# Two stores moved behind five DMA transposes in SyncE's queue, and one buffer moved from one pool tag to another

## The chip, the cores and the metric

The kernel runs on one core of one Trainium2 chip. The metric is the device time of one execution in microseconds. The profile names the core's engines PE (TensorE matmuls; PEld are its weight loads), DVE (VectorE), ACT (ScalarE), POOL (GpSimd) and SP (SyncE, which only issues DMAs here). "SPq" is SyncE's queue of instructions, and a DMA "lands" when its semaphore reports that all of its data has been written.

## The reference

Sliding-window causal attention over 8 batches of 8 heads, 576 positions and 64 channels, and after it a feed-forward layer with the gate h cos(h) over all 4608 rows.

```python
scores = scale * np.matmul(q, k.transpose(0, 1, 3, 2))       # window of 64 positions, causal
attn = exp(scores - max); attn = attn / sum(attn)
x = matmul(attn, v)        # (8, 8, 576, 64), then rows of 512: (4608, 512)
h = x @ w_in               # 512 -> 2048
out = (h * np.cos(h)) @ w_out   # 2048 -> 512, float32
```

## The kernel before, in words

The 4608 rows are nine tiles of 512 rows (`MT`), numbered 0 to 8. One batch is nine blocks of 64 positions, so a tile of eight blocks straddles batches. For each tile the kernel runs, on TensorE, the second attention product (`values`, L428: `o_ps` from the transposed weights `wT` and `v`), the first feed-forward product (L496: `h_ps`, 256 matmuls in bf16), and the second one (L747: `out_ps`, and for the last three tiles a form with fewer products, L585). ScalarE takes the sine of `h_ps` (L731), VectorE multiplies (L734).

Between these, in the same stage, lies the attention of a later batch. TensorE makes the scores in two bursts (`burst_scores`, L327). For each group of four score blocks VectorE subtracts the mask and finds the maximum (`g_max`, L364), ScalarE exponentiates (`g_exp`, L376), VectorE takes the reciprocal of the sum (`g_inv`, L386), GpSimd or, for some groups, VectorE writes the normalised weights `w` (`g_norm`, L393), and a DMA transpose from SyncE's queue turns them into `wT` (`g_trans`, L412). A few groups are transposed on TensorE instead (L409, copied by VectorE). There are nine groups in the stage of a tile. In the stage of tile 2 five of them are written and transposed one after the other in its second half, and the five results are read by `values` of tile 3 at the stage's end; the other four follow.

The rest of the DMA work of a stage: GpSimd issues the loads of `q`, `k` and `v` (L186, L192). SyncE issues, besides the weight transposes, the transposes of whole batches of q and k (`turn_q`, `turn_k`, L243, three DMAs each, the "turns"), and two stores of 512 KB per tile (`store`, L505), each with 256 finished rows.

The order is written out by hand. Up to tile 0 it is a list of steps (`FIRST`). From tile 1 on a plan holds steps with a time: `at(time, fn, ...)` puts a step in, `pump(time)`, called after each piece of the matmuls, runs the steps due by then. The times are in units of the program, `T` = 32 of them to a tile; they order the instructions and are no microseconds. Each engine runs its own instructions in the order in which they were recorded; what they wait for are semaphores that follow from the tiles that they read and write.

Two pool tags matter. `out` holds the finished rows, 256 rows to a buffer: `load_plain` borrows two buffers at the start, each tile takes two (L740), and a buffer may be written again when the store that reads it has landed. `w` holds a group of normalised weights; its buffer may be written again when the transpose that reads it is done. The buffers of a tag are taken in rotation, three for `out` (`OUTS`, L40) and eight for `w` (L391).

Of the kernel before, what the change touches and what calls it, by code (L numbers as in the profile page):

```python
# [15 lines left out]
BF16 = mybir.dt.bfloat16  # L16
# [9 lines left out]
GF = 4  # L26
# [9 lines left out]
T = 2 * Q  # L36
LAGS = (0.2, 1, 3, 3.2, 3.8)
SKEW = 3
DIRECT = (0, 7, 8)
OUTS = 3  # L40
FILL = (6, 12)
BUSY = 8
NB = 5
# [31 lines left out]
def kernel(  # L75
# [23 lines left out]
    att = ctx.enter_context(tc.tile_pool(name="att", bufs=3))  # L99
# [26 lines left out]
    def bank(which, name):  # L126
        return ps.tile([128, 512], F32, tag=which, name=name)

    def copy(engine, out, in_):
        {"a": nc.scalar.copy, "p": nc.gpsimd.tensor_copy}.get(engine, nc.vector.tensor_copy)(out, in_)  # L130
# [40 lines left out]
    def load_plain(name):  # L171
        rows = moe.tile([128, 2, d_model], F32, tag="out", name="rows", bufs=OUTS).rearrange("p a f -> p (a f)")[:, 0:RC * D]
        st["rows", name] = rows
        nc.sync.dma_start(out=rows, in_={"q": q, "k": k}[name][0, 0:2].rearrange("h (p c) d -> (h p) (c d)", c=RC))
# [213 lines left out]

    def g_norm(n, engine="p"):
        (e, _), rden = st.pop(("e", n)), st.pop(("r", n))  # L390
        w = att.tile([128, GF, 128], BF16, tag="w", name="w", bufs=8)  # L391
        u = len(groups[n])
        (nc.gpsimd if engine == "p" else nc.vector).tensor_tensor(out=w[:, 0:u], in0=e[:, 0:u], op=ALU.mult,  # L393
                                in1=rden[:, 0:u].unsqueeze(2).to_broadcast([128, u, 128]))
        st["w", n] = w
# [86 lines left out]
    def put_out(m, engine=None):  # L482
        if ("osb", m // 2) not in st:
            st["osb", m // 2] = moe.tile([128, 2, d_model], F32, tag="out", name="out_sb", bufs=OUTS)
        copy(engine, st["osb", m // 2][:, m % 2], st.pop(("out", m)))

    def exp_table():
        nc.scalar.activation(small, small, AF.Exp, scale=0.0)
# [4 lines left out]
    def first(mt, ff, ks, start, stop):  # L493
        if start:
            st["h", ff] = bank(H_BANKS[mt == 1][ff], "h_ps")
        nc.tensor.matmul(out=st["h", ff], lhsT=w_in_sb[:, ks, ff * 128:ff * 128 + 128],  # L496
                         rhs=st["xT", mt][:, ks], start=start, stop=stop)

    def skewed(mt, ks, n):
        for ff in range(SKEW):  # L500
            first(mt, ff, ks, n == 0, n == PAIRS - 1)

    def store(o_sb, mt, ms0, e, n):
        r0 = mt * MT + (ms0 + e) * 128
        nc.sync.dma_start(out=out[r0:r0 + n * 128].rearrange("(a p) f -> p a f", p=128), in_=o_sb[:, e:e + n])  # L505
# [21 lines left out]
    def plan_rows(mt, gT):  # L527
        t = mt * T
        for f in range(4):
            at(t + (8 + 0.1 * f if mt == FAST[0] else 2 * f + 1.2), sum_row, 2, f, gT, "p")  # L530
            for i in range(2):
                at(t + (11, 13, 14.62, 14.7)[f] + 0.01 * i, sum_row, i, f, gT, "d")
            at(t + (18 if mt == FAST[0] else 17.7) + 0.01 * f, sum_row, 3, f, gT, "d")
        if mt < n_mt - 1:
            at(t + T - 0.505, sine_table)

    def fast_second(mt, gT):
# [7 lines left out]
        acc, temp = {}, {}  # L545
        o1, o2 = (moe.tile([128, 2, d_model], F32, tag="out", name="out_sb", bufs=OUTS) for _ in range(2))

# [51 lines left out]
    def at(time, fn, *args):  # L599
        plan.append((time, len(plan), fn, args))  # L600

    def pump(time):
        plan.sort(key=lambda x: x[:2])
        while plan and plan[0][0] <= time:
            _, _, fn, args = plan.pop(0)
            fn(*args)


    for i, (b, jobs, banks) in enumerate(bursts):
        t = T * (b - 1)  # L610
        at(t + (BURST[i % 2] + 0.9 * (i == 1) if b < B - 1 else (17.2, T + 14.6)[i % 2]), burst_scores, i)
        for n in range(jobs[0][0], jobs[-1][-1] + 1):
            place = (n - n_listed) % NU
            time = t + BURST[0] + PACE * place
            if b == B - 1:
                for time, fn in zip(LAST_STEPS[place], (g_max, g_exp, g_inv, g_trans)):
                    at(t + time, fn, n)
                at(t + LAST_STEPS[place][2] + 0.01, g_norm, n, "p")
                continue
            lags = LAGS[:2] + tuple(t + T - 0.79 - time + 0.01 * s for s in range(3)) if place == NU - 1 else LAGS  # L620
            if b == 2 and place > 3:
                lags = tuple(max(x, y - time) for x, y in zip(lags, {4: (53.2, 53.5, 0, 0, 0), 5: (0,) * 5, 6: (0, 0, 60.96, 60.97, 61.5), 7: (0, 0, 61.1, 61.2, 61.8), 8: (61, 61.3, 0, 0, 0)}[place]))
            for lag, fn in zip(lags, (g_max, g_exp, g_inv)):
                at(time + lag, fn, n)
            at(time + lags[3], g_norm, n, "d" if n == n_listed + 5 else "p")
            if n in last:
                at(T * b - 4.1 + (n == last[1]), g_trans, n)
                at(T * b - 4.05 + (n == last[1]), g_put, n)
            else:
                at(time + lags[4], g_trans, n)  # L630
# [51 lines left out]
    def spread_first(lo, hi):  # L682
# [16 lines left out]
             "s": lambda p, g, which: g_scores(2 * p + g, which), "m": lambda p, g: g_max(2 * p + g),  # L699
             "e": lambda p, g: g_exp(2 * p + g), "i": lambda p, g: g_inv(2 * p + g),  # L700
             "n": lambda p, g, engine: g_norm(2 * p + g, engine), "w": lambda p, g: g_trans(2 * p + g),
             "c": lambda p, g, engine: g_put(2 * p + g, engine), "v": values_half, "x": put_x_half,
             "tb": sine_table, "tb2": exp_table, "h": first_half, "S": sine_half, "g": gate_half,
# [9 lines left out]
    for mt in range(1, n_mt):  # L713
        base = mt * T
        gT = []
        if mt in FAST:
            plan_rows(mt, gT)
        for ks in range(PAIRS):
            pump(max([base - 1] + [time for time, _, fn, args in plan if fn is put_x and args[:2] == (mt, ks)]))
            skewed(mt, ks, ks)  # L720
        for ff in range(n_ff):
            for ks in range(PAIRS):
                if ff >= SKEW:
                    first(mt, ff, ks, ks == 0, ks == PAIRS - 1)
            h_ps = st.pop(("h", ff))
            sin = moe.tile([128, MT], F32, tag="sin", name="sin", bufs=4)
            if ff % 2 == 0:
                gt = moe.tile([128, 2, MT], BF16, tag="gT", name="gT", bufs=n_ff // 2 + 2)
                gT.append(gt)
            e = ff % 2  # L730
            nc.scalar.activation(sin, h_ps, AF.Sin, bias=math.pi / 2.0)  # L731
            if ff == n_ff - 1 and mt < B:
                exp_table()
            nc.vector.tensor_tensor(out=gt[:, e], in0=h_ps, in1=sin, op=ALU.mult)  # L734
            pump(base + ff)
        if mt in FAST:
            fast_second(mt, gT)
            continue
        for ms0 in range(0, MT // 128, 2):
            o_sb = moe.tile([128, 2, d_model], F32, tag="out", name="out_sb", bufs=OUTS)  # L740
            o_ps = [bank(which, "out_ps") for which in (("O1",) if mt == n_mt - 1 and ms0 else ("O1", "O0"))]
            for e in range(2):
                ms = ms0 + e
                for ff in range(n_ff):
                    if e and ms0 and ff == n_ff - 1 and 0 < mt < FAST[0]:
                        pump(base + T - 0.6)
                    nc.tensor.matmul(out=o_ps[e], lhsT=gT[ff // 2][:, ff % 2, ms * 128:ms * 128 + 128],  # L747
                                     rhs=w_out_sb[:, ff], start=ff == 0, stop=ff == n_ff - 1)
                    if ff % 4 == 3:
                        if ff == n_ff - 1:  # L750
                            copy("a" if e and (mt > 1 or ms0) else "d", o_sb[:, e], o_ps[e])
                            if mt == n_mt - 1:
                                store(o_sb, mt, ms0, e, 1)
                        pump(base + Q + 4 * ms0 + (e * n_ff + ff) // 4)
            if mt < n_mt - 1:
                at(base + T + 0.5 + ms0 / 2, store, o_sb, mt, ms0, 0, 2)


# [28 lines left out]
```

## Time and profile before

| | |
|---|---|
| runs shown | 299.11, 299.21, 297.6 us, median 299.11 |
| profiled execution, its own time | 296.92 us |
| its span | 295.2 us |
| granted TensorE clock | 1.00 throughout |
| DMA queues, share of 16 engines over the span | GpSimd's 83.5%, SyncE's 46.7% |
| HBM read, written | 36.70 MB, 9.44 MB |

Times inside the profile count from the start of the span. The stages of tiles 2, 3 and 4 begin at 87.01, 118.27 and 148.66 us. A row of the timeline gives the start, the length, engine and line, and what was written from what; behind it, in brackets, how long the engine had been idle and what ended that. A row of the DMA view gives what moved, the queue, how many issues the window holds, the size of one and the time from issue to landing.

### The profile page before, as it was taken

The numbers are of one execution on the slowest core, as the hardware profiler recorded it, in microseconds if no ns is written. First come the engines' busy times: TensorE is split into PE (matmuls) and PEld (weight loads), VectorE is DVE, ScalarE is ACT, GpSimd is POOL, SyncE is SP. The second block draws the span as 40 slices with busy tenths as digits, with TensorE's granted clock in tenths as the row PEclk, the third lists the DMA queues.
The fourth block names the chain that finished last, engine by engine and source line by source line (L and its number), as shares of the span: only waits on it lengthen the run. The fifth ranks groups of instructions, "written<-read, shape, count | busy, mean of one in ns | idle before, by whom it ended". The sixth has DMA issues, their size and how long they took to land.

```text
span 295.2 us, 8262 instructions
## 1 busy us (share of the span) xinstructions
PE 285.3 (97%) x2786; PEld 163.2 (55%) x2815; DVE 230.3 (78%) x906; ACT 238.0 (81%) x791; POOL 209.7 (71%) x230
## 2 busy tenths in 40 slices
PE   8979999999999999999999999999999999999995
PEld 3668854544454444444454545444547854884595
DVE  4998888887887876788678876996689878957853
ACT  5998699888987798879987999799977896937710
POOL 9999568992899759984999399948995476133200
PEclk9999999999999999999999999999999999999999
DMA  7999999999999999999999999999959415042013
GB/s 149 174 201 205 196 191 143 141 143 155 203 197 120 162 235 154 155 163 232 168 142 158 235 155 145 147 213 185 141 122 200 45 38 178 2 117 83 0 38 107
DMA packets 168267, 43.81 MB, mean 148 GB/s; under 512 B 155616, under 2 KB 163872, under 8 KB 168224
## 3 DMA queue, kind: packets, MB, share of 16 engines
q0 software_dynamic: 100896, 18.06, 83.5%
q1 hardware_dynamic: 67184, 25.15, 46.7%
q8 instruction: 22, 0.36, 0.5%
q14 instruction: 21, 0.17, 0.2%
q10 hardware_dynamic: 144, 0.07, 0.1%
HBM read 36.70 MB, written 9.44 MB: 156 GB/s over the span
## 4 chain that ended last, share of the span: by engine, by line
PE 86%; POOL 5%; ACT 3%; DMA 2%; issue 2%; DVE 1%; POOLq 0%
PE h_ps L496 38%; PE out_ps L747 18%; PE out_ps L585 13%; PE h_ps L460 5%; PE out_ps L479 5%; PE o_ps L428 3%; ACT e L376 2%; PE s_ps L327 2%; DMA wT<-w 2%; POOL v L192 1%; POOL q L169 1%; POOL k L169 1%; POOL w L393 1%; PE tw_ps L409 1%; PE s_ps L349 1%
## 5 line engine op out<-in xcount | busy, mean ns | idle before, releaser
L496 PE MATMUL h_ps<-xT,w_in 128*128 128x512 bf16 x502 | 111.3, 379 | 1.3 <-DVE xT L130 0.8
L393 POOL TENSOR_TENSOR w<-e,rden 128x512 bf16<-128x512 f32 (+1 forms) x68 | 69.2, 1030 | 48.6 <-DVE rden L386 38.6
L734 DVE TENSOR_TENSOR gT<-h_ps,sin 128x512 bf16<-128x512 f32 x128 | 84.6, 687 | 21.8 <-ACT sin L731 20.4
L376 ACT ACTIVATE e<-s,negm 128x128 f32<-128x128 f32 (+1 forms) x256 | 97.2, 382 | 2.6 <-DVE negm L364 1.6
L731 ACT ACTIVATE sin<-h_ps 128x512 f32<-128x512 f32 x128 | 73.6, 599 | 25.4 <-PE h_ps L496 23.5
L496 PEld LDWEIGHTS <-w_in 128*128 128x128 bf16 x512 | 50.2, 98 | 59.3
L747 PE MATMUL out_ps<-w_out,gT 128*128 128x512 bf16 x305 | 68.7, 379 | 1.1 <-issue 0.8
L364 DVE CUSTOM_DVE_ANT_0 s<-s_ps,mask 128x128 f32<-128x128 f32 (+1 forms) x256 | 55.8, 277 | 1.9 <-PE s_ps L349 1.6
L747 PEld LDWEIGHTS <-gT 128*128 128x128 bf16 x320 | 30.4, 98 | 35.5
L376 ACT ACTIVATION_READ_ACCUMULATOR e<-s,negm 128x1 f32 x256 | 48.0, 188 | 0.0
L192 POOL DMA_DIRECT2D v<-in_v_dram x40 | 34.1, 874 | 1.0 <-issue 0.9
L186 POOL DMA_DIRECT2D q<-in_q_dram x30 | 26.3, 894 | 3.6 <-issue 3.0
L186 POOL DMA_DIRECT2D k<-in_k_dram x30 | 26.3, 887 | 0.0
L386 DVE RECIPROCAL rden<-den 128x4 f32<-128x4 f32 (+1 forms) x73 | 12.0, 165 | 17.2 <-ACT e L376 16.8
L130 POOL COPY v<-v 64x1536 bf16<-64x1536 bf16 (+3 forms) x16 | 22.9, 1431 | 0.4
L364 DVE DVE_READ_ACCUMULATOR2_ANT negm<- 128x1 f32 x256 | 21.2, 83 | 0.0
L525 POOL TENSOR_TENSOR qT<-gT 128x512 bf16<-128x512 bf16 x12 | 13.6, 1154 | 9.1 <-DVE gT L734 9.0
L130 DVE CAST xT<-o_ps 128x512 bf16<-128x512 f32 x24 | 15.5, 680 | 5.8 <-PE o_ps L428 5.5
L585 PEld LDWEIGHTS <-gT 128*128 128x128 bf16 x152 | 14.0, 98 | 2.2
L460 PE MATMUL h_ps<-xT,w_in 128*128 128x256 bf16 x128 | 14.6, 273 | 0.0
L479 PE MATMUL out_ps<-w_out,gT 128*128 128x512 bf16 x60 | 14.3, 380 | 0.3 <-issue 0.2
L556 DVE TENSOR_TENSOR out_sb<-out_ps,p 128x512 f32<-128x512 f32 (+2 forms) x16 | 8.6, 548 | 6.7 <-ACT p L130 5.6
(90 smaller groups left out, 327.0 us busy)
## 6 DMA issues: line engine op xcount, KB each, us to landing
out_dram<-out_sb SPq DMA_DIRECT2D x16, 512.0 KB, 8.2
v<-in_v_dram POOLq DMA_DIRECT2D x32, 128.0 KB, 5.8
q<-in_q_dram POOLq DMA_DIRECT2D x24, 128.0 KB, 8.5
k<-in_k_dram POOLq DMA_DIRECT2D x24, 128.0 KB, 7.1
w_in<-in_moe_w_in_dram POOLq DMA_DIRECT2D x4, 512.0 KB, 9.4
w_out<-in_moe_w_out_dram POOLq DMA_DIRECT2D x4, 512.0 KB, 11.0
q<-in_q_dram POOLq DMA_DIRECT2D x7, 144.0 KB, 5.7
k<-in_k_dram POOLq DMA_DIRECT2D x7, 144.0 KB, 5.8
```

Of the source, the lines that this page charges most:

```text
L130: {"a": nc.scalar.copy, "p": nc.gpsimd.tensor_copy}.get(engine, nc.vector.tensor_copy)(out, in_)
L186: nc.gpsimd.dma_start(out=st[name, b][0:n, c].rearrange("p (h d) -> p h d", h=H), in_=src.rearrange("h p d -> p h d"))
L192: nc.gpsimd.dma_start(out=vt.rearrange("p (h d) -> p h d", h=H), in_=v[b, :, c * 128:c * 128 + n, :].rearrange("h p d -> p h d"))
L364: nc.vector.tensor_tensor_reduce(out=s[:, u, c], in0=s_ps[:, u, c], in1=mask[:, 2 - j % 2 if j else 0, c], scale=-scale if b else -1.0, sc ...
L376: nc.scalar.activation(e[:, u, c], s[:, u, c], AF.Exp, bias=negm[:, u:u + 1], scale=1.0 if n < n_first else -1.0, accum_out=den[:, u:u + 1])
L393: (nc.gpsimd if engine == "p" else nc.vector).tensor_tensor(out=w[:, 0:u], in0=e[:, 0:u], op=ALU.mult, in1=rden[:, 0:u].unsqueeze(2).to_br ...
L460: nc.tensor.matmul(out=h_ps[:, half * e:half * e + half], lhsT=w_in_sb[:, ks, ff * 128:ff * 128 + 128], rhs=st["xT", 0][:, ks, half * g:ha ...
L496: nc.tensor.matmul(out=st["h", ff], lhsT=w_in_sb[:, ks, ff * 128:ff * 128 + 128], rhs=st["xT", mt][:, ks], start=start, stop=stop)
L585: nc.tensor.matmul(out=to[n_] if split else to[:, e], lhsT=lhs[name][f // 2][:, f % 2, 128 * e:128 * e + 128], rhs=rhs[name][:, f, lo:hi], ...
L731: nc.scalar.activation(sin, h_ps, AF.Sin, bias=math.pi / 2.0)
L734: nc.vector.tensor_tensor(out=gt[:, e], in0=h_ps, in1=sin, op=ALU.mult)
L747: nc.tensor.matmul(out=o_ps[e], lhsT=gT[ff // 2][:, ff % 2, ms * 128:ms * 128 + 128], rhs=w_out_sb[:, ff], start=ff == 0, stop=ff == n_ff - 1)
```

## The change

The two stores of tile 1 get another time in the plan. Before, `at` gave them 0.5 and 1.5 units behind the end of tile 1's stage; now 24.2 and 24.22 units behind it, late in tile 2's stage. The other tiles' stores keep theirs. `out` gets four buffers in place of three and `w` seven in place of eight.

```diff
-OUTS = 3
+OUTS = 4
...
-        w = att.tile([128, GF, 128], BF16, tag="w", name="w", bufs=8)
+        w = att.tile([128, GF, 128], BF16, tag="w", name="w", bufs=7)
...
             if mt < n_mt - 1:
-                at(base + T + 0.5 + ms0 / 2, store, o_sb, mt, ms0, 0, 2)
+                at(base + T + (24.2 + 0.01 * ms0 if mt == 1 else 0.5 + ms0 / 2), store, o_sb, mt, ms0, 0, 2)
```

In SyncE's queue this is the stretch from the turns at the start of tile 2's stage to the turns for the batch after it. `wT<-w` are the weight transposes, the first three for the groups of the stage before, the next five those of tile 2's stage; `out_dram<-out_sb` are the stores.

```order
 L243 DMA_TRANSPOSE kT<-k 128x8x128 x2
 L243 DMA_TRANSPOSE kT<-k 128x4x64
-L412 DMA_TRANSPOSE wT<-w 128x4x128 x3
+L412 DMA_TRANSPOSE wT<-w 128x4x128 x8
 L505 DMA out_dram<-out_sb 128x2x512 x2
-L412 DMA_TRANSPOSE wT<-w 128x4x128 x5
 L243 DMA_TRANSPOSE qT_75<-q 128x8x128 x2
 L243 DMA_TRANSPOSE qT_75<-q 128x4x64
```

The two stores have moved behind the five transposes and stand directly ahead of the turns of q. This is the only difference in the order of any engine.

What instructions wait for changes in more places, since the buffers rotate otherwise. On VectorE, at the end of the written-out first part (two groups of batch 1 whose `w` VectorE writes itself), the rows with their semaphores are these; `DMAHW5` and `DMAHW6` count the landings of the first and the second weight transpose of the program.

```order
 L386 RECIPROCAL rden<-den 128x3 [waits Activation_49]
-L393 TENSOR_TENSOR w<-e,rden 128x384 [waits DVE_49]
-L384 MEMSET e 128x64 [waits Pool_49]
-L386 RECIPROCAL rden<-den 128x4 [waits Activation_49]
-L393 TENSOR_TENSOR w<-e,rden 128x512 [waits DMAHW5_49,DVE_49]
+L393 TENSOR_TENSOR w<-e,rden 128x384 [waits DMAHW5_49,DVE_49,Pool_49]
+L384 MEMSET e 128x64 [waits Pool_49]
+L386 RECIPROCAL rden<-den 128x4 [waits Activation_49]
+L393 TENSOR_TENSOR w<-e,rden 128x512 [waits DMAHW6_49,DVE_49]
 L130 COPY wT<-tw_ps 128x512 [waits PE_49]
 L130 COPY wT<-tw_ps 128x384 [waits PE_49]
```

The order is the same; each of the two writes now waits for one transpose later than before: the first, which waited for none, for the first, and the second for the second.

## The prediction

> **What bounds the kernel now.** I read the page first, then each tile's stage on its own, then the chain of waits around the one stage that is longer than its neighbours. The page says that TensorE is the bound.
>
> ```profile
> span 295.2 us, 8262 instructions
> PE 285.3 (97%) x2786; PEld 163.2 (55%) x2815; DVE 230.3 (78%) x906; ACT 238.0 (81%) x791; POOL 209.7 (71%) x230
> ```
>
> The span less the busy time leaves TensorE 9.9 us idle, so a change of the order of DMAs can gain only where TensorE waits for one. The windows of the stages of tiles 2, 3 and 4, each from the first h_ps matmul of a tile to that of the next (columns: window, its length, busy us and instruction count of each engine, granted clock, DMA share, GB/s), show where that is.
>
> ```profile
> 87.01:118.27 31.26, 30.34 (x261) 14.67 (x265) 23.14 (x109) 27.20 (x95) 26.19 (x29) 1.00 1.74 163
> 118.27:148.66 30.39, 29.97 (x260) 14.48 (x264) 23.21 (x109) 27.18 (x95) 24.69 (x27) 1.00 1.71 178
> 148.66:179.05 30.39, 29.97 (x260) 14.51 (x264) 23.18 (x109) 27.06 (x95) 25.00 (x27) 1.00 1.83 169
> ```
>
> Tiles 3 and 4 take 30.39 us; tile 2 takes 31.26, at the same clock of 1.00. The excess is 0.87 us. The chain of waits tells what ends last there (start, length, what):
>
> ```profile
> 110.91 1.05 POOL w L393
> ...
> 111.97 5.11 DMA wT<-w
> ...
> 117.13 0.98 PE o_ps L428 x50
> ...
> 147.37 1.13 PE o_ps L428 x64
> ```
>
> In tile 3's stage the 64 small o_ps matmuls run as one piece of 1.13 us. In tile 2's, TensorE stands still twice for a transposed weight block (the timeline; the bracket holds the idle time and what ended it):
>
> ```profile
> 116.04 0.38 PE L428 MATMUL o_ps<-wT,v 128*64 128x64 bf16 x11
> 116.61 0.22 PE L428 MATMUL o_ps<-wT,v 128*64 128x64 bf16 x3 [0.20 <-DMA wT<-w]
> 117.13 0.98 PE L428 MATMUL o_ps<-wT,v 128*64 128x64 bf16 x50 [0.29 <-DMA wT<-w]
> ```
>
> The last wait ends with the fifth weight transpose of the stage, which took 5.11 us from its issue at 111.97 to its landing.
>
> **The change: the two stores.** SyncE's queue in this stage and the next (start, length, what, how many):
>
> ```profile
> 100.55 1.10 SPq L505 DMA_DIRECT2D out_dram<-out_sb  x2
> 105.92 7.24 SPq L412 DMA_TRANSPOSE wT<-w  x5
> 113.33 5.58 SPq L243 DMA_TRANSPOSE qT<-q  x3
> 119.75 2.01 SPq L412 DMA_TRANSPOSE wT<-w  x1
> 121.87 4.73 SPq L243 DMA_TRANSPOSE kT<-k  x3
> 126.69 4.29 SPq L412 DMA_TRANSPOSE wT<-w  x3
> 131.08 1.15 SPq L505 DMA_DIRECT2D out_dram<-out_sb  x2
> ```
>
> The two stores, 1 MB together, stand ahead of the five transposes and will stand behind them. SyncE itself idles from 101.65 to 105.92, so their issue delays nothing today. Their data do. The DMA view of the windows around each issue gives the time to landing of the two stores, of the first transpose and of the fifth:
>
> ```profile
> out_dram<-out_sb SPq DMA_DIRECT2D x1, 512.0 KB, 8.6
> out_dram<-out_sb SPq DMA_DIRECT2D x1, 512.0 KB, 9.6
> wT<-w SPq DMA_TRANSPOSE x1, 7.1
> wT<-w SPq DMA_TRANSPOSE x1, 5.1
> ```
>
> The stores land at about 109.2 and 110.9 (100.55 + 8.6, 101.22 + 9.6), the first transpose only at 113.0 (105.92 + 7.1), the fifth at 117.1. They land in order. Two cuts through the DMA queues (packets, MB, share of 16 engines; q1 is SyncE's queue, q0 GpSimd's), for 105.3 to 109.2 and for 113 to 117:
>
> ```profile
> q1 hardware_dynamic: 614, 1.04, 82.2%
> q0 software_dynamic: 1012, 0.13, 50.3%
> ...
> q1 hardware_dynamic: 2177, 0.53, 140.6%
> q0 software_dynamic: 82, 0.01, 4.0%
> ```
>
> In the first 3.9 us q1 moves the stores' 1.04 MB and nearly nothing else, though transposes are issued from 105.92 on. In the second, q0 is empty and q1 works off the transposes. With the stores behind, the transposes find their queue free when issued, and the stores fall into the stretch in which q0 is empty.
>
> The Trainium skill ("DMA: Bandwidth & Descriptors", section "Queues, rings and completion order") says that each DMA engine takes the descriptors of one queue row in ring order, and changes between rows packet by packet. By that rule the transposes must wait for the stores of their own row, and the landings above agree; if an engine took turns within a row too, the move would be worth nothing and the sum would stay at 296.92.
>
> How early can the fifth land? It cannot be issued before GpSimd has written its block: that ends at 111.96 on the chain, whatever the stores do. So the gain hangs on its landing time alone. The nearest rows are the last transpose of the same run of blocks in tile 3's stage (issued at 141.69, itself behind two stores) and in tile 4's (issued at 172.14), and the extremes of all 60:
>
> ```profile
> 141.69 1.19 SPq L412 DMA_TRANSPOSE wT<-w  x1
> ...
> wT<-w SPq DMA_TRANSPOSE x1, 3.8
> wT<-w SPq DMA_TRANSPOSE x1, 2.5
> DMA to landing us min/median/max: 2.4/5.1/8.8
> ```
>
> TensorE reaches the block after 14 of its 64 matmuls, 14/64 of 1.13 = 0.25 us after 116.04: at 116.29, which is 4.3 us after the issue. At 3.8 us or less nothing waits; at an unchanged 5.1 it still waits 0.8. I take 3.8, since that transpose too had a store pair close ahead of it and three of its own kind; the bounds are 2.4 and 5.1. The second to fourth blocks are issued 4.4 to 1.4 us earlier and come first. The stage then lasts as long as tile 3's, to 87.01 + 30.39 = 117.40 in place of 118.27. **Gain: 0.87 us** (bounds 0.1 to 0.9).
>
> What is late next? The next stages run at 30.39 without a wait for DMA, so they begin 0.87 us earlier and keep it, unless the moved stores hurt them. Behind the stores now stand the three qT turns, one weight transpose and three kT turns. Their issue slips by 1.1 us, their data by up to the stores' 3.9. Their first user is the burst of scores of the next stage; its second part needs the last kT turn (its issue, its time to landing, and the two parts):
>
> ```profile
> 124.68 1.92 SPq L243 DMA_TRANSPOSE kT<-k  x1
> ...
> kT<-k SPq DMA_TRANSPOSE x1, 6.6
> 132.17 0.59 PE L327 MATMUL s_ps<-kT,qT 64*64 64x64 bf16 x32
> 137.98 0.86 PE L327 MATMUL s_ps<-kT,qT 64*64 64x128 bf16 x40
> ```
>
> The turn lands at 131.3, needed at 137.98 - 0.87 = 137.1: 5.8 us of cover against 3.9. The first part needs only the first turns of q and k, issued at 113.33 and 121.87, over ten us earlier. **Cost: nothing**; without that cover it would be up to 3.9 us. GpSimd's and ScalarE's queues issue the same in the same order.
>
> **Four row buffers, seven weight buffers.** With three row buffers tile 2's second pair would be copied into the buffer that tile 1's first store reads. With four, tile 1's buffers are needed next by tile 3, whose first copy stands here:
>
> ```profile
> 136.82 0.69 DVE L130 COPY out_sb<-out_ps 128x512 f32<-128x512 f32 x1
> ```
>
> A store issued at about 113.2 that takes as long as 9.6 us lands at 123: 13 us of cover. Nothing gained either, since today no copy waits for a store.
>
> With seven weight buffers a block waits for the transpose of the seventh before it, not the eighth. In the stages above these are most of a stage apart. It is close only at the end of the written-out first part, where VectorE writes two blocks and now waits there for the first and the second DMA transpose of the program (the run of six from 43.13, of which the second is issued at 44.45; then the second's time to landing, and the two VectorE blocks):
>
> ```profile
> 43.13 8.85 SPq L412 DMA_TRANSPOSE wT<-w  x6
> ...
> wT<-w SPq DMA_TRANSPOSE x1, 7.1
> ...
> 51.36 0.73 DVE L393 TENSOR_TENSOR w<-e,rden 128x384 bf16<-128x384 f32 x1
> 52.23 0.69 DVE L393 TENSOR_TENSOR w<-e,rden 128x512 bf16<-128x512 f32 x1
> ```
>
> The second lands at 51.55, 0.68 us before VectorE needs it; the first has no landing in the trace, but stands ahead in the queue, so it is there by 51.55, at the worst 0.2 us late. Behind these two in VectorE's queue are the copies that feed tile 1's first matmuls, so the cost is 0 to 0.2 us. I take 0, since 0.87 us separate the two VectorE blocks and 1.3 the two issues, which puts the first at about 50.3.
>
> Sum: the profiled execution took 296.92 us for a span of 295.2. 296.92 - 0.87 + 0 + 0 = 296.05. The three runs shown are 297.6 to 299.21, median 299.11; the profiled one lies below them all, so I take the difference to the median: 299.11 - 0.87 = **298.2 us**.
>
> **The rivals.**
>
> *The wait stays.* The transposes between 113 and 117 may be slow by themselves: there q1 needs 140.6% for 0.53 MB, where the stores needed 82.2% for 1.04 MB. If the fifth takes 5.1 us with a free queue too (the median of all 60), TensorE waits to 117.09 as now. For it speaks that median; against it the 3.8 and 2.5 at the same place of the next stages. Gain 0 to 0.1: 299.0 us. Chance 0.22.
>
> *The stores are paid for one stage later: slower.* The DMA engines are busy nearly throughout, so 3.9 us of stores, put behind, may push everything in q1 until tile 3's four blocks arrive late. The fourth lands at 141.69 + 3.8 = 145.5 and is needed 0.2 us into the o_ps that starts at 147.37, less 0.87: at 146.7. Cover 1.2 us. A full push of 3.9 makes TensorE wait 2.7: 299.11 - 0.87 + 2.7 = 300.9. It turns into a loss from a push of 1.2 + 0.87 = 2.1 us on. Against it: q0's 4.0% between 113 and 117 is a hole that the stores fill, and what q0 lost to them before 109 it gets back. Chance 0.10. The Trainium skill (same page, "Issuing engines are not separate DMA queues") says that DMAs from all issuing engines end on the same 16 engines and interleave, so that an order moves work and saves none; by it alone this rival would come first.
>
> *The shorter ring of weight buffers bites.* The cover of 0.68 us is one execution's. If the first transposes land 1 to 2 us later in others, VectorE stalls by 0.3 to 1.3 us ahead of tile 1: 299.11 - 0.87 + 0.3 to 1.3 = 298.5 to 299.5. Chance 0.08.
>
> **How the numbers follow.** The forecast has 0.60. A measurement of this kernel tells about 0.5% from no change, 1.5 us; no case gains that much, and only a strong push of the stores, over 2.1 + 1.5 = 3.6 us, loses it. The runs shown differ by 1.6 us among themselves, which I count as 0.12 for faster by over 0.5%. Slower gets half of the second rival and a rest, 0.06; within 0.5% keeps 0.82. Low end: the lowest run less the gain is 296.7, the profiled one less it 296.05; between them, 296.4. High end: the highest run with the buffer rival's loss, 299.21 + 0.4, and a part of the push: 299.9.
>
> **What would show it.** Right: tile 2's stage at 30.4 us, the five transposes at 2.4 to 4.3 us, no wait of o_ps for wT, the stores issued at about 113 and landing by 120, later stages at 30.39. Wrong: a stage of 31.2 with the fifth still at 5 us; a stage of tile 3 above 30.4 with o_ps waiting for wT or s_ps for kT; VectorE idle ahead of its two blocks near 52 us.

## The result, and the profile after

The changed kernel is slower. Six runs took 300.16 to 301.34 us, median 301.16, and six runs of the kernel before, recorded with them, had a median of 298.13: a ratio of 1.009, 95% interval 1.0062 to 1.0117. Here and below a ratio leaves out runs over 1.5% above the fastest of the same kernel and a median does not, so the two need not agree where such runs fall out (three of 12 with four loads, one of 12 in three other runs, and some of the kernel before). The forecast was 298.2 with a range up to 299.9. The rival in which the stores are paid for one stage later had been priced at 300.9 and given a chance of 0.10.

The page of the changed kernel shows 4.1 us more span (299.3 for 295.2). By it TensorE is busy for 4.7 us more (285.3 before) and idle for about as long as before.

```profile
span 299.3 us, 8285 instructions
PE 290.0 (97%) x2815; PEld 164.3 (55%) x2815; DVE 229.8 (77%) x906; ACT 238.2 (80%) x791; POOL 209.9 (70%) x230
```

This page alone would mislead, since matmul records are missing from a trace (2815 here, 2786 before), so the busy times of the two pages do not compare to a microsecond. The windows of the stages of tiles 2, 3 and 4, cut as before from the first h_ps matmul of a tile to that of the next, do (window, length, busy us and count of each engine, granted clock, DMA share, GB/s).

```profile
87.25:117.64 30.39, 30.39 (x265) 14.49 (x264) 23.14 (x109) 27.20 (x95) 25.33 (x28) 1.00 1.59 153
117.64:152.36 34.72, 31.67 (x265) 15.30 (x264) 23.91 (x111) 27.65 (x95) 29.52 (x32) 0.96 1.75 164
152.36:183.17 30.81, 30.81 (x265) 14.63 (x264) 22.51 (x107) 26.85 (x94) 21.15 (x23) 0.99 1.76 172
```

Tile 2's stage went from 31.26 to 30.39, the forecast gain of 0.87 us to the hundredth. Tile 3's went from 30.39 to 34.72, tile 4's to 30.81. The sum is -0.87 + 4.33 + 0.42 = +3.88; tile 2's stage also began 0.24 later, which no part of the change explains (in most of the runs below it begins 0.1 to 1.4 us later too), and together that is the 4.1.

TensorE at the end of tile 3's stage, in the timeline (start, length, what, how many, and in brackets the idle time before and what ended it):

```profile
146.67 0.69 PE L428 MATMUL o_ps<-wT,v 128*64 128x64 bf16 x12
148.48 0.19 PE L428 MATMUL o_ps<-wT,v 128*64 128x64 bf16 x1 [1.12 <-DMA wT<-w]
150.48 1.55 PE L428 MATMUL o_ps<-wT,v 128*64 128x64 bf16 x51 [1.81 <-DMA wT<-w]
```

It waits for two transposed blocks, 1.12 + 1.81 = 2.93 us. The 64 o_ps matmuls themselves take 0.69 + 0.19 + 1.55 = 2.43 us, where the piece quoted before took 1.13: 1.30 more. Of that 0.45 is what being broken up costs at a full clock: in tile 2's stage of the kernel before, with two waits in it, the same piece took 0.38 + 0.22 + 0.98 = 1.58 us. The rest is the clock. The 0.96 of the stage's row is an average: windows laid on the pieces give a granted clock of 1.00 for the first twelve matmuls and of 0.50 for the last 51, and 0.50 still from 152.03 to 152.57. Waits and slower matmuls make 4.23 of the 4.33 us; the other 0.1 is about what the half clock costs from 152.03 to the stage's end. The chain of waits through the same place (start, length, what) names the block, and shows the half clock go on into the next product, where 64 matmuls take 14.19 us for 13.83 in the stage before:

```profile
117.80 13.83 PE h_ps L496 x64
...
140.06 1.04 POOL w L393
...
141.89 8.54 DMA wT<-w
...
150.48 1.55 PE o_ps L428 x51
152.03 0.54 PE out_ps L747
152.57 14.19 PE h_ps L496 x64
```

The block was issued at 141.89, 0.2 us later than before (141.69), but took 8.54 us to land in place of 3.8. So GpSimd, which had written it by 141.10 (before: 141.66), is not late, and SyncE, which issues the transpose, hardly: the data are. SyncE's queue from the moved stores to that block:

```profile
97.41 16.05 SPq L412 DMA_TRANSPOSE wT<-w  x7
114.00 0.89 SPq L505 DMA_DIRECT2D out_dram<-out_sb  x2
115.06 6.95 SPq L243 DMA_TRANSPOSE qT<-q  x3
122.10 1.21 SPq L412 DMA_TRANSPOSE wT<-w  x1
123.41 5.57 SPq L243 DMA_TRANSPOSE kT<-k  x3
129.08 4.24 SPq L412 DMA_TRANSPOSE wT<-w  x3
133.42 1.12 SPq L505 DMA_DIRECT2D out_dram<-out_sb  x2
136.56 8.19 SPq L412 DMA_TRANSPOSE wT<-w  x4
```

The turns are issued 1.5 to 2.9 us later than before and the last kT turn lands at 134.8 (131.3 before), still ahead of its use. The two moved stores and the fifth transposition of tile 2's stage (DMA view) landed quickly, as forecast (3.8 us is the middle of 3.2 and 4.5):

```profile
out_dram<-out_sb SPq DMA_DIRECT2D x2, 512.0 KB, 3.8
...
wT<-w SPq DMA_TRANSPOSE x1, 2.4
```

What the prediction did not look at is the DMA engines' own row. For 109.5 to 114.5 us the DMA view gives the busy share of the 16 engines in 40 slices of 0.125 us, in tenths, and the queues' shares below it; first the kernel before, then the changed one.

```profile
DMA  9999999999999999999999999999999998910999
...
q0 software_dynamic: 2393, 0.30, 93.7%
q1 hardware_dynamic: 1782, 0.45, 84.8%
```

```profile
DMA  9999911099996999910699995000000199996100
...
q1 hardware_dynamic: 2484, 0.60, 86.2%
q0 software_dynamic: 68, 0.01, 2.9%
```

Before, no slice but three is below 9. After, there are holes. Counting a 9 as full and a digit d as (9.5 - d) tenths of a slice idle, the engines idle 0.24 us before and 1.91 us after. While the stores had gone first, GpSimd's loads (q0) had waited beside them and then filled the time in which q1 had little; with the stores held back, q0 is finished (2.9%), and q1 has nothing but transposes, each of which waits for GpSimd to write its block.

A second hole lies in tile 3's stage. This is the row from 135.25 to 139.25 in the changed kernel, in slices of 0.1 us; in the kernel before, 135.01 to 139.01 is 9 throughout:

```profile
DMA  9999999999999999999990001101115999999999
```

Counted in the same way, 135.25 to 143.25 holds 1.21 us of idle time, where 135.01 to 143.01 before holds 0.09, and this although tile 2's two stores had been issued at 133.42 and 134.08. They land at about 142.6 and 144.2. Before, they had landed by 141.2, ahead of the issue of the fourth block; now it is issued with their data still in its queue. GpSimd's loads, too, were out of the way before and are in it now (q0 for 143.01 to 147.01 before, then for 143.25 to 147.25 after):

```profile
q0 software_dynamic: 2, 0.00, 0.1%
...
q0 software_dynamic: 1552, 0.20, 76.9%
```

### The profile page after: what moved, and what is told of

Read it like the earlier page. It is cut to its first block, busy times and chain, and to the rows that moved or that the text cites. A ratio compares the mean times of both kernels' runs of the same rounds, so it can differ in the third digit from the quotient of the medians.

```text
span 299.3 us, 8285 instructions
## 1 busy us (share of the span) xinstructions
PE 290.0 (97%) x2815; PEld 164.3 (55%) x2815; DVE 229.8 (77%) x906; ACT 238.2 (80%) x791; POOL 209.9 (70%) x230
## 4 chain that ended last, share of the span: by engine, by line
PE 87%; ACT 7%; DMA 3%; issue 1%; DVE 1%; POOL 0%; POOLq 0%
PE h_ps L496 37%; PE out_ps L747 19%; PE out_ps L585 12%; ACT e L376 5%; PE out_ps L479 5%; PE h_ps L460 4%; PE o_ps L428 3%; DMA wT<-w 3%; PE s_ps L327 2%; PE busy L137 1%; PE s_ps L349 1%; ACT kT L130 1%; PE tw_ps L409 0%; ACT L491 0%; PE tk_ps L225 0%
## 5 line engine op out<-in xcount | busy, mean ns | idle before, releaser
L496 PE MATMUL h_ps<-xT,w_in 128*128 128x512 bf16 x512 | 112.2, 380 | 0.0
L747 PE MATMUL out_ps<-w_out,gT 128*128 128x512 bf16 x320 | 72.2, 380 | 0.0
L747 PEld LDWEIGHTS <-gT 128*128 128x128 bf16 x320 | 30.4, 98 | 35.5
L479 PE MATMUL out_ps<-w_out,gT 128*128 128x512 bf16 x64 | 14.8, 380 | 0.0
L428 PE MATMUL o_ps<-wT,v 128*64 128x64 bf16 x512 | 11.0, 201 | 3.1 <-DMA wT<-w 2.9
```

Source lines behind the costliest of these rows:

```text
L479: nc.tensor.matmul(out=st["out", m], lhsT=st["g", ff // 2][:, ff % 2, m * 128:m * 128 + 128], rhs=w_out_sb[:, ff], start=ff == 0, stop=ff ...
```

## The experiments

Two theories run through the experiments. **Gap** (on record from the first run on): the stores are held behind a transpose that waits for GpSimd, so the DMA engines run dry around 109.5 to 114.5 us, and that lost time comes back as late weight transposes in tile 3's stage. **Slip** (on record from the fifth run on): it is only how late the 1 MB enters q1; the loss grows with it. Two more were on record and tested first: **buffer** (the rotation of the rings costs it) and **place** (the stores stand directly ahead of the turns). Each run was timed beside the kernel before; ratios are to that kernel.

**The buffers alone**, on the kernel before:

```diff
-OUTS = 3
+OUTS = 4
-        w = att.tile([128, GF, 128], BF16, tag="w", name="w", bufs=8)
+        w = att.tile([128, GF, 128], BF16, tag="w", name="w", bufs=7)
```

> Four row buffers and seven weight buffers, the stores at their old place. Gap theory (with the stores held behind the fifth weight transpose the DMA queues run dry from about 109.5 to 114.5 us, and the lost DMA time comes back as late weight transposes in tile 3's stage) and place theory (the stores hurt because they stand directly ahead of the turns): as before, 298.1 us, ratio 1.000 +- 0.003, tile 2's stage 31.2 us, tile 3's 30.4. Buffer theory (the shorter ring of weight buffers or the new addresses cost the time): about 301, with tile 3's stage above 31.

Measured: 297.39 us, 0.9986 (0.9959 to 1.0013). Tiles 2 and 3 have the stages of the kernel before:

```profile
87.16:118.50 31.34, 30.34 (x261) 14.62 (x264) 23.13 (x109) 27.21 (x95) 26.23 (x29) 1.00 1.69 162
118.50:148.89 30.39, 29.97 (x260) 14.49 (x264) 23.20 (x109) 27.18 (x95) 24.59 (x27) 1.00 1.70 178
```

The buffers cost nothing; the buffer theory falls.

**The changed kernel without tile 1's stores**; 512 rows of the output are left unwritten:

```diff
-            if mt < n_mt - 1:
+            if mt < n_mt - 1 and mt != 1:
```

> The changed kernel without tile 1's two stores: 512 rows of the output are left out, 1 MB less is moved. Gap and place theory: tile 2's stage 30.4 us; tile 3's blocks land before they are needed, so tile 3's stage is 30.4 to 31 and the time 297.0 to 297.9, ratio about 0.997. Buffer theory: tile 3's stage stays at 34 to 35 us, 301.

Measured: 297.31 us, 0.9974 (0.9942 to 1.0005).

```profile
87.90:118.28 30.38, 29.96 (x260) 14.44 (x264) 23.13 (x109) 27.19 (x95) 25.27 (x28) 1.00 1.63 133
118.28:148.68 30.40, 29.98 (x261) 14.52 (x265) 23.21 (x109) 27.20 (x95) 25.56 (x28) 1.00 1.83 177
```

```profile
DMA  9999111110999999999100006999830000001899
```

Both stages are at 30.4. So the whole loss comes from the 1 MB in its new place, and the gain of tile 2's stage is real. It also shows that a hole by itself need not hurt: by the last row, the tenths from 109.5 to 114.5, the engines idle 2.21 us in the same stretch here. By the gap theory it hurts once the work that could have filled it has still to be done.

**The stores behind the kT turns** (place says that this mends it), on the changed kernel:

```diff
-                at(base + T + (24.2 + 0.01 * ms0 if mt == 1 else 0.5 + ms0 / 2), store, o_sb, mt, ms0, 0, 2)
+                at(base + T + (26.45 + 0.01 * ms0 if mt == 1 else 0.5 + ms0 / 2), store, o_sb, mt, ms0, 0, 2)
```

> The changed kernel with tile 1's stores moved further back, behind the turns of q and k of the same stage. Place theory: the turns land early again, what is left to push are the last three weight blocks and tile 2's stores, and tile 3's stage falls to 30.4 to 32 us, 297 to 299. Gap theory: nothing more fills the gap and 1 MB still waits in front of tile 3's four blocks, so tile 3's stage stays at 34 us or more, 301 or above.

Measured: 304.3 us, 1.0242 (1.0176 to 1.0308), the slowest of all, from four runs; the profiled one, at 301.81, is the fastest of them. Tile 3's stage:

```profile
117.50:152.97 35.47, 31.23 (x261) 15.44 (x264) 23.91 (x111) 27.64 (x95) 29.51 (x32) 0.97 1.80 186
```

The place theory falls: the turns were not what suffered, and the later the stores, the more is lost.

**Two loads in the gap.** Two loads of k for batch 4, which GpSimd issues at about 115.5, are issued at about 102, so that q0 has work in the stretch; on the changed kernel, and as a control on the kernel before. The line picks the loads that are put late in the stage, and now leaves out those two:

```diff
-                    if name == "k" and (b == 3 or c > 2):
+                    if name == "k" and (b == 3 or c > 2 and b != 4):
```

> The changed kernel with two of GpSimd's loads of k, which it issues at 115.5 us after its copies, issued at about 102 us, ahead of the five weight blocks: 192 KB in 1536 packets that can be moved in the gap. Gap theory: about 1.3 us of DMA time is saved (1536 packets at 16 engines and about 1190 packets per us), tile 3's stage falls from 34.8 to about 33 us or less and the time to 299 to 300. Place theory: the stores stand where they stood, tile 3's stage stays at 34.5 to 35, 301.

> The kernel before, with the two loads of k issued at about 102 us in place of 115.5, the stores where they were: the control for the run with the loads in the gap. Gap theory: there the stores already fill the time from 105 to 109, the loads only crowd it and leave 113 to 117 emptier, so nothing is gained: ratio 0.998 to 1.005. If the loads gain by themselves whatever the stores do: ratio 0.996 or less, since they took 0.004 off the changed kernel.

Measured: on the changed kernel 299.4 us, 1.0051 (1.0017 to 1.0086); on the kernel before 300.45 us, 1.0068 (1.0029 to 1.0108). Stages of tiles 2, 3 and 4 with the changed kernel, and the hole there:

```profile
88.12:118.51 30.39, 29.96 (x261) 14.44 (x264) 23.14 (x109) 27.21 (x95) 26.80 (x30) 1.00 1.93 159
118.51:149.46 30.95, 30.16 (x261) 14.59 (x265) 23.22 (x109) 27.43 (x95) 24.62 (x26) 1.00 1.68 171
149.46:181.93 32.47, 30.27 (x260) 14.67 (x264) 23.21 (x109) 27.27 (x95) 26.61 (x29) 1.00 1.82 164
```

```profile
DMA  9999999999111110699999999128999820000029
...
q1 hardware_dynamic: 2293, 0.55, 91.2%
q0 software_dynamic: 759, 0.09, 31.1%
```

Alone, the early loads lose 0.7%, more than the gap theory had allowed (up to 1.005); in their profile TensorE waits 2.2 us for weight blocks at the end of tile 2's stage. The stores held back lose 0.9%. If the two losses had nothing to do with each other, both edits together would lose 1.6%; they lose 0.5%, at most 0.86%. So the two losses are not independent, which neither slip nor place foresees; that the loads take something off the changed kernel's own loss is not clear of noise, since 1.0017 to 1.0086 and 1.0062 to 1.0117 overlap. Nor do the loads fill the hole: 1.71 us are still idle, and from 109.5 to 119.5 the engines idle 2.75 us with them and 2.59 without. Part of the push only moved on, to tile 4's stage (32.47).

**Four loads in the gap.** As above, and the first loads of q and k of batch 5 too, all on the changed kernel:

```diff
-                        time = (24.26 if b == 5 else 22.46) + 0.01 * i - T
+                        time = (13 if b == 5 else 22.46) + 0.01 * i - T
```

> The changed kernel with four loads (448 KB, 3584 packets) issued ahead of the five weight blocks in place of two: the second dose. Gap theory: 3 us of DMA time is used before the gap in place of 1.3, so the loss shrinks further: ratio 1.000 to 1.004, tile 3's stage 30.4 to 31.5. Slip theory (only the lateness of the stores counts): they stand where they stood, ratio 1.009, tile 3's stage above 34.

Measured: 299.19 us, 1.0017 (0.9977 to 1.0057). In its profile the stretch from 109.5 to 114.5 has no hole:

```profile
DMA  9999999999999999999999999999999997899999
...
q0 software_dynamic: 4974, 0.62, 230.6%
q1 hardware_dynamic: 461, 0.12, 18.0%
```

But the hole is not filled, it comes later. The extra loads hold GpSimd up (between their issues it waits up to 1.71 us for earlier loads to land), so that it writes the five blocks from 111.6 to 116.6 in place of 105.1 to 112.2; the row from 116.44 to 120.44 has 2.02 us of idle time, and the stores are issued at 119.65, later than the 114.00 of the changed kernel:

```profile
DMA  2899999300000299999620000027999973000300
...
119.65 0.89 SPq L505 DMA_DIRECT2D out_dram<-out_sb  x2
```

The profiled execution was 3.5 us over the median, so its stages are not read here, and whether the other executions have the same holes is not known. Slip, which wanted 1.009 for stores as late, falls by the interval of the ratio (the medians of all runs, 299.19 and 297.8, would give 1.0047). That the loss shrinks because a hole is filled is not shown by this run.

**How much, and how late.** Four runs on the changed kernel. Two put both stores behind the second or the fourth transposition (19.9 or 22.75 in place of 24.2), one puts only the second store behind the fifth and leaves the first in its old place, and one moves the first ahead of the kT turns as well. The lines that stand in place of the changed one, in this order:

```diff
+                at(base + T + (19.9 + 0.01 * ms0 if mt == 1 else 0.5 + ms0 / 2), store, o_sb, mt, ms0, 0, 2)
...
+                at(base + T + (22.75 + 0.01 * ms0 if mt == 1 else 0.5 + ms0 / 2), store, o_sb, mt, ms0, 0, 2)
...
+                at(base + T + (24.2 if mt == 1 and ms0 else 0.5 + ms0 / 2), store, o_sb, mt, ms0, 0, 2)
...
+                at(base + T + ((24.2 if ms0 else -6.1) if mt == 1 else 0.5 + ms0 / 2), store, o_sb, mt, ms0, 0, 2)
```

> The changed kernel with tile 1's stores behind the second of the five weight transposes, issued at about 110 us. Gap theory: the stores' data fill the time in which the third to fifth block wait for GpSimd, the queues do not run dry, the fifth block lands at 115 to 116.5; tile 2's stage 30.4 to 30.8 us, tile 3's 30.4, ratio 0.996 to 0.999. Slip theory (the loss grows with how late the 1 MB is issued: 13 us of slip gave 1.009, so 9 us give two thirds of it): tile 3's stage above 32 us, ratio about 1.006.

> The changed kernel with tile 1's stores behind the fourth of the five weight transposes, issued at about 112 us. Gap theory: half of the gap is left, tile 2's stage 30.4 to 31, tile 3's 31 to 33.5, ratio 1.000 to 1.006. Slip theory: 11.5 us of slip, tile 3's stage about 34, ratio about 1.008.

> The changed kernel with only the second store behind the fifth weight transpose, the first at its old place. Gap theory: 0.5 MB fills the time from 105 to 107.5, half of the engine time is lost, and the fifth transpose has half the data ahead of it: tile 2's stage 30.4 to 30.8, tile 3's 30.4 to 32, ratio 0.998 to 1.005. Slip theory: half of the bytes slip, ratio 1.004 to 1.005, tile 3's stage above 32.

> Both edits at once: tile 1's first store ahead of the kT turns of tile 2's stage, its second behind the fifth transposition; between the two places q1 holds the transpositions alone. Gap theory: half of the stores fills the earlier stretch, half the later one, so tile 2's stage takes 30.4 us, tile 3's 30.4, and the time is 0.995 to 0.999 of before, no lower than the better of the two edits alone (0.9972, 0.9976) by more than 0.002, since tile 2's wait of 0.87 us can be saved only once. Slip theory (what counts is how late the data are): half of the data are as late as in the changed kernel, 1.002 to 1.005, with tile 3's stage at 30.8 to 32.5.

Measured, with the idle time of the engines in 109.5 to 114.5, counted as above from the same row of each profile:

| tile 1's stores | idle, us | stages of tiles 2, 3, 4, us | ratio (95%) |
|---|---|---|---|
| old place (before) | 0.24 | 31.26, 30.39, 30.39 | 1 |
| second behind the fifth | 0.17 | 30.38, 30.40, 30.39 | 0.9976 (0.9943 to 1.0009) |
| first early, second behind the fifth | 0.61 | 30.39, 30.40, 31.24 | 1.0003 (0.9973 to 1.0033) |
| both behind the second | 0.90 | 31.26, 30.40, 30.39 | 1.0040 (1.0012 to 1.0067) |
| both behind the fourth | 1.43 | 31.68, 30.94, 30.39 | 1.0066 (1.0045 to 1.0087) |
| both behind the fifth (the change) | 1.91 | 30.39, 34.72, 30.81 | 1.0090 (1.0062 to 1.0117) |
| both behind the kT turns | 2.38 | 30.39, 35.47, 30.96 | 1.0242 (1.0176 to 1.0308) |

With one store in the old place there is hardly a hole in the row, and no stage waits:

```profile
DMA  9999999999999999944899999999999899999999
```

```profile
87.67:118.05 30.38, 29.96 (x260) 14.49 (x264) 23.13 (x109) 27.18 (x95) 25.27 (x28) 1.00 1.70 162
118.05:148.45 30.40, 29.98 (x261) 14.48 (x265) 23.23 (x109) 27.20 (x95) 25.56 (x28) 1.00 1.68 181
```

The loss goes with the idle time, down the whole table, and also when the 5 us are laid as far behind the start of each profile's own stage. It does not when the stretch is made longer: from 109.5 to 119.5 the engines idle 0.66, 0.79, 1.39, 2.53, 1.87, 2.59 and 3.33 us down the table, so that both stores behind the second leave as much idle time as the change and lose less than half as much. Nor outside the table: the early loads alone and the stores from ScalarE (below) lose 0.7% with no idle slice in the 5 us.

Slip expected 1.004 to 1.005 for the second store alone, and the measured interval ends at 1.0009. But a push against a cover, without any gap, would do the same: by the prediction's own figures half of the data pushes by 1.95 us, and a loss begins at 2.1.

The gap theory missed three forecasts here. For the split it expected 0.995 to 0.999, and measured are 1.0003 and a wait in tile 4's stage. For both stores behind the fourth it expected 30.4 to 31 and 31 to 33.5 us in tiles 2 and 3, and at most 1.006. For both behind the second it expected 0.996 to 0.999, on the ground that the gap would be small. In that profile another cost shows. SyncE issues one DMA after the other, and the stores take 1.05 us of it in the middle of the run of transposes, so that the fifth is issued at 115.88, 2.61 us after GpSimd has written its block (before: 0.01 us after); it lands in 2.5 us, and tile 2's stage is as long as before (31.26):

```profile
97.29 13.20 SPq L412 DMA_TRANSPOSE wT<-w  x4
110.58 1.05 SPq L505 DMA_DIRECT2D out_dram<-out_sb  x2
111.73 5.36 SPq L412 DMA_TRANSPOSE wT<-w  x3
```

The profile thus explains why nothing is gained; that the runs lose 0.4% it does not show.

**Another queue.** On the kernel before, tile 1's stores are issued by ScalarE, at about 97 us:

```diff
-        nc.sync.dma_start(out=out[r0:r0 + n * 128].rearrange("(a p) f -> p a f", p=128), in_=o_sb[:, e:e + n])
+        (nc.scalar if mt == 1 else nc.sync).dma_start(out=out[r0:r0 + n * 128].rearrange("(a p) f -> p a f", p=128), in_=o_sb[:, e:e + n])
...
-                at(base + T + 0.5 + ms0 / 2, store, o_sb, mt, ms0, 0, 2)
+                at(base + T + (9 if mt == 1 else 0.5) + ms0 / 2, store, o_sb, mt, ms0, 0, 2)
```

> The kernel before with tile 1's two stores issued from ScalarE's queue among the sines at about 96 us, three row buffers and eight weight buffers. Their data share the engines with SyncE's transposes and GpSimd's loads in place of standing ahead of them in one queue. Gap theory: no time of the DMA engines is lost and the five transposes have SyncE's queue to themselves: tile 2's stage 30.4, tile 3's 30.4, ratio 0.996 to 0.999. Slip theory: not later than before, so no loss either; it names no gain.

Measured: 298.96 us, 1.0065 (1.0037 to 1.0093); here too the gap theory's forecast was wrong. No hole appears from 109.5 to 114.5 (0.0 us idle), but the fifth weight transpose gets slower, and tile 2's stage waits (its window, and the block on the chain of waits):

```profile
88.10:121.95 33.85, 30.50 (x261) 14.73 (x265) 23.14 (x109) 27.22 (x95) 28.74 (x32) 1.00 1.84 148
```

```profile
113.89 6.87 DMA wT<-w
```

The block in question takes 6.87 us where it took 5.11 behind the stores in one queue. The stores are not beside it any more: issued at 96.94 and 97.80, they took 9.7 and 11.8 us and had landed by 109.6, before the block was issued. What it meets is GpSimd's loads, which moved 0.52 MB from 109.5 to 114.5 (0.30 MB before). The Trainium skill says in "DMA: Bandwidth & Descriptors", section "Issuing engines are not separate DMA queues", that DMAs of all issuing engines run on the same 16 engines and interleave, and that starting them from several engines saves only the time of issue; this run agrees in so far as nothing was gained (1.0065).

**Earlier in place of later**, on the kernel before: both stores earlier (the first ahead of the kT turns at about 88 us, the second at about 97, and the second and third kT turns of batch 3 later), or the first store alone. The first two lines are the run with both, the last that with the first alone.

```diff
+            at(t0 + 0.1 * lo - (2 if b == 2 else 0.3 if b == 3 and lo else 6), turn_k, b, lo, hi)
+                at(base + T + ((-0.9 if ms0 else -6.1) if mt == 1 else 0.5 + ms0 / 2), store, o_sb, mt, ms0, 0, 2)
...
+                at(base + T + (-6.1 if mt == 1 and not ms0 else 0.5 + ms0 / 2), store, o_sb, mt, ms0, 0, 2)
```

> The kernel before with tile 1's first store ahead of the turns of k at the start of tile 2's stage, the second behind the three weight transposes there and ahead of the second and third turn of k: issued at about 87 and 92 us, where the DMA engines move little. Three row buffers, eight weight buffers. Gap theory: DMA time that is unused today is used, so the five transposes land 2 to 5 us earlier and everything behind is earlier too: tile 2's stage 30.4, tile 3's 30.4, ratio 0.995 to 0.998, and the slowest of the runs of before (above 300) become rarer. Rival: the turns of k or the loads behind them are pushed instead, a scores burst waits, tile 2's stage stays above 31, ratio 1.000 or more.

> The kernel before with only tile 1's first store moved forward, ahead of the turns of k at about 87 us, where the DMA engines move little; the second stays. Three row buffers, eight weight buffers. Gap theory: half of the stores' data leaves the stretch from 105 to 109, the fifth transpose lands 1 to 1.4 us earlier, nothing stands behind: tile 2's stage 30.4 to 30.7, tile 3's 30.4, ratio 0.995 to 0.998. Rival: the first store holds up the turns of k, as both did in some executions of the run with both early, and tile 2's stage stays above 31: ratio 1.000 or more.

Measured: both 296.66 us, 0.9982 (0.995 to 1.0015); the first alone 297.19 us, 0.9972 (0.9935 to 1.0008). Of the 12 runs with both early, eight took 295.9 to 296.8 and four 298.2 to 299.8. The profiled execution is one of the four; the chain has a kT turn there that takes 11.66 us to land, and tile 2's stage is 32.33 us. So with both stores early most executions lie 1 to 1.9 us below the median of the kernel before (297.77) and the others 0.5 to 2 us above it; the gap theory had forecast 0.995 to 0.998 and a stage of 30.4. (With the first store alone the profiled execution was over 5 us above the median and is not read.) None of the three best versions (this, the first alone, the second store alone late) is clear of 1.

## Why the prediction was wrong

*Tile 2's wait goes: right.* Fifth transposition in 2.4 us (forecast 2.4 to 4.3), stage 30.39, gain 0.87. That it hung on its landing time and that the stores in its queue made it late holds as well, with one limit: with the stores taken to another queue it was later still, at 6.87 us.

*Four row buffers, seven weight buffers: right*, both at nothing (0.9986 with them alone).

*"Cost: nothing" behind the stores: wrong, and this is the step that failed.* The cover of 5.8 us was that of the turns; they were issued 1.5 to 2.9 us later (forecast 1.1), landed 2.4 to 5.2 us later, and nobody waited for them. But the lateness does not end with them, it is handed on to what q1 takes later: tile 2's stores land 3 us later, and the fourth block of tile 3 landed at 141.89 + 8.54 = 150.4, in place of 145.5. That is a push of 4.9 us, against a cover that the rival itself put at 1.2. The push also exceeds what I took as its upper bound, 3.9. The row that I had read as "itself behind two stores" was not: before, those stores had landed by 141.2, and the block was issued at 141.69.

*The reason under it: "the stores fall into the stretch in which q0 is empty".* q0 being empty is not a hole in the engines. In the cut from 113 to 117 that I quoted, q1 alone had 140.6%; and in the stretch just ahead of it the row of tenths of the kernel before has hardly an idle slice. The engines were nearly full before: with the stores in their old place, GpSimd's loads were left over for the time in which the transposes waited for GpSimd. The rival had this sentence ("busy nearly throughout") and I gave it 0.10 where the DMA row should have made it the first case. The section of the Trainium skill quoted there ("DMA: Bandwidth & Descriptors", "Issuing engines are not separate DMA queues") states that DMAs of all issuing engines run on the same 16 engines and interleave; what the rival concluded from it, that an order moves work and saves none, was the better guide.

*The rival's price.* A full push gave a wait of 2.7 and 300.9 us; measured were waits of 2.93, and 301.16. The near agreement is luck in part: the broken-up o_ps matmuls at half clock, and the half clock behind them (1.30 + 0.42 us), which I had not priced, stand against a median of before that was 1 us lower in these runs. The push was mis-sized too (4.9 for 3.9).

What is shown: the 1 MB in the new place is the cause (the loss is gone without the stores), not the buffers and not the neighbourhood of the turns; lateness in proportion to the data is out too (half of the data as late costs nothing). The path is shown in the trace, from the late block to TensorE's waits and the half clock behind them. That idle engine time is what is paid back is argued, not shown: the table's order speaks for it, but it hangs on where the 5 us are cut, and the run with four loads, meant to fill the hole, only moved it. As a sum it does not close either: in the profile of the changed kernel the two holes hold 3.05 us more idle time than the kernel before (1.93 from 109.5 to 119.5, 1.12 in the second), against a push of 4.9. GpSimd's loads, which now run beside the fourth block, are a candidate for the rest that no run prices. Why the engines stood idle near 138 us with two stores issued stays open, and so do the six forecasts that the gap theory missed in whole or in part (behind the second, behind the fourth, split, loads alone, ScalarE's queue, both early).

## What to carry to other kernels

Before a transfer is moved out of the way of an urgent one, look at the busy row of the DMA engines, not at one queue's share: here it was nearly full, and a queue's low share (q0's 4.0%) was no room for the stores. A wait that is saved in one stage must be checked against the smallest cover anywhere downstream in the same queue, up to the point where the queue runs empty, not against the next user alone. Half of the transfer may fit where all of it does not, as one store of the two did here.

## What the runs showed of the hardware

The granted clock went to half after short pauses. In the changed kernel TensorE stood idle for 1.12 and 1.81 us within 4 us, and windows give a clock of 0.89 for 149 to 150, 0.50 from 150 to 153, 0.80 for 153 to 153.5 and 1.00 after that: by these rows (an estimate) some 3.4 us at half, from 149.8 to 153.2, which began inside the second pause. Half clock for 1.88 us in tile 3's stage and 0.85 us in tile 4's costs 0.94 and 0.42 us, and 64 matmuls of h_ps took 14.19 us for 13.83. The sum of the pauses does not decide it. With the stores from ScalarE, TensorE waits 0.78, 1.75 and 0.40 us in much the same span, 2.93 in all as here, and with the two early loads once for 1.78 us, and both rows keep 1.00; with the early loads alone, waits of 1.19, 0.81 and 0.20 us end in a clock of 0.50. What decides is not shown.

The time to landing of the same transpose (512 columns of 128 rows) ran from 2.4 us, in a stretch with holes, to 8.54 us in the backlog; a store of 512 KB took 3.2 and 4.5 us in the new place and 8.6 and 9.6 in the old.
